# The turn between the second and the third stage of an FFT convolution: inside SBUF from GpSimd's queue instead of through DRAM

## The chip, the cores and the metric

One core of one Trainium2 chip. The metric is the device time of one execution in microseconds, and the runs of a kernel are compared by their median. "The profile" is one execution as the hardware profiler recorded it: a summary page, and a trace that can be asked for groups of instructions, waits, transfers and stretches of time. Engines: PE is TensorE (PEld its weight loads), DVE is VectorE, ACT is ScalarE, POOL is GpSimd, SP is SyncE; SPq, ACTq and POOLq are the sequencers of those engines when they only issue a transfer.

## The reference

Shapes: `u` is 2048 x 512 (time by channel), 512 channels with 128 states each, a hidden layer of 1792. All float32.

```python
x = A_u
g = sigmoid((x * gate_w).sum(-1, keepdims=True))
# a: a long convolution per channel, with a kernel made of 128 complex exponentials
dt = exp(log_dt)[:, None]
P = exp(dt * (A_re + 1j*A_im))[..., None] ** arange(L)
K = einsum("dn,dnl,dn->dl", C_re + 1j*C_im, P, dt * (B_re + 1j*B_im)).real
a = irfft(rfft(u, 2*L) * rfft(K, 2*L))[:L] + u * Dskip
# b: a dense layer with gelu, and one back
b = gelu(x @ w1 + b1) @ w2 + b2
return g * a + (1 - g) * b
```

## The kernel before, in words

The work has two parts. The first, `front` (0 to 397 us), makes the convolution kernel's samples, takes the first stage of the Fourier transforms of signal and kernel into DRAM (`tu_d`, `tk_d`), and computes the dense branch, whose gated results are added into the output in DRAM. A planner orders its instructions. Two of the sixteen row tiles of the dense branch (the last N_LATE = 2 of the block treated last, tiles 2 and 3) are not finished there: their 14 groups of three products (a product with the high parts, and two with the low parts) are kept in the list `late`.

The second, `conv` (from 397 us), has an order written out by hand. It treats 32 frequencies, two in each of 16 steps `s`. In a step:

- `product(s)`: six VectorE operations multiply the transformed signal (`pu`, in PSUM) by the transformed kernel (`k0`, `k1`, in SBUF).
- `signal(s+1)` and `taps(s+2)`: eight TensorE products each for the coming steps; ScalarE copies the taps out of PSUM.
- `inverse(s)`: eight TensorE products (line 1158) give `pa`, for each of the two frequencies `n` a tile of 128 rows by 512 channels. A row is one of 64 samples, real or imaginary.
- `turn(s)`: ScalarE copies `pa` to one of six tiles `sa` in SBUF (line 1164), and the turn begins.

The turn exchanges rows for columns. The third stage sums over frequencies, so the frequencies have to lie on partitions: `t3` has 128 partitions (32 frequencies, real and imaginary, two halves) of 32 samples x 512 channels, 64 KB each. Before the change the turn goes through DRAM: SP writes each `sa` into `t4_d` (line 1167, 256 KB), and after every GROUP = 8 frequencies GpSimd's queue reads the group back into 32 partitions of `t3`, in four transfers of 512 KB (line 1176). The last group is read back in eight transfers of 256 KB from SP and ACT, and the write of frequency 31 is issued by ACT.

`seat(n)` says on which partition frequency `n` sits; the constants (`g1` for the third stage, `g2` for the inverse stage) are laid out to fit. `matrices(m)` makes from a loaded constant tile the second set of weights (`f1`, `g1`) with four ScalarE instructions (lines 1103 to 1106); it serves two steps.

While the steps run, `fetch` and `load_u` load the taps and the signal (SP), and from step 6 on `dense(k)` loads the dense results of output block k back from DRAM (SP, line 1186, 512 KB).

Behind step 15:

- `rest(n)` issues the next `n` groups of the late list (lines 1197 to 1199). One group (N_REST) stands ahead of the last `inverse`, 13 behind it.
- A dummy product (`warm`, line 1235), then for the two late tiles a VectorE operation that gates and adds them (line 1239).
- Eight final blocks, one for each pair of output tiles `m`: sixteen TensorE products (line 1247) with the weights `g1t` give two PSUM tiles `pb`. A block reads four of the 32 samples of all the partitions of `t3`, so it needs every frequency, but of each only an eighth of its row. Eleven of the sixteen tiles are gated and added to the dense result by VectorE in one operation (line 1258); five (those in ASIDE) by ScalarE (line 1255) and GpSimd (line 1256). Each pair is then stored: 512 KB from SP (line 1262), the first and the last pair in two halves (line 1260).

Waits are put in by the framework from what the instructions read and write.

Of the kernel before, what the change touches and what calls it, by code (L numbers as in the profile page):

```python
# [9 lines left out]
F32 = mybir.dt.float32  # L10
# [3 lines left out]
ALU = mybir.AluOpType  # L14
# [3 lines left out]
P = 128  # L18
L = 2048
# [51 lines left out]
D_COE = 1.413  # L71
D_OUT = -13.28
N_REST = 1
N_KEEP = 1
N_PASS = 20
N_LATE = 2

N_ATTIC, N_LOFT, N_TK = 11, 8, 8
N_US = N_ATTIC + N_LOFT
W_DVE = ((1, 0), (3, 0), (5, 0))  # L80

GROUP = 8

ASIDE = (2, 4, 7, 9, 12)
PI = float(np.pi)
TWO_PI = 2.0 * PI
TURN = 2.0**32
# [13 lines left out]
    return [8 * (n % 4) + n // 4 for n in range(32)]  # L101


def seat(n):

    return 4 * (n % 8) + n // 8


def constants():


    def om(e4):
# [12 lines left out]


    rows = np.zeros((2, 64, 32))
    for n, k in enumerate(k0_order()):
        rows[:, seat(n)] = er.T[k] / L
        rows[:, seat(n) + 32] = ei.T[k] / L  # L130
    g1 = rows.reshape(P, 32)

    ko = k0_order()
    f2 = np.zeros((32, 2, 64, 64))
    g2 = np.zeros((32, 64, 64, 2))
    for n, k in enumerate(ko):
        er, ei = om(4 * (q[:, None] * k + 32 * np.outer(q, k1)) + q[:, None])
        f2[n, 0], f2[n, 1] = er, -ei  # L140
        er, ei = om(4 * (qn[None] * k + 32 * np.outer(k1, qn)) + qn[None])
        g2[n, :, :, 0], g2[n, :, :, 1] = er, -ei
# [153 lines left out]
def gated_mix(  # L296
# [21 lines left out]
    dr = ctx.enter_context(tc.tile_pool(name="dr", bufs=1, space=DRAM))  # L318

    dt_d = dr.tile([1, D], F32, name="dt_d")  # L320
    t4_d = dr.tile([4, 2, 2, GROUP, 32, D], F32, name="t4_d")
    tu_d = dr.tile([2, 32, 2, 64, D // 2], F32, name="tu_d")
    tk_d = dr.tile([2, 32, 2, 64, D // UW, 64], F32, name="tk_d")

# [753 lines left out]
    def conv(pool, ps, late, attic, loft):  # L1078
# [17 lines left out]
        def matrices(m):  # L1096

            cc = c4s[m]
            f = cc[:, 0].rearrange("p (n k) -> p n k", n=4)
            f1 = pool.tile([P, 4, 64], F32, tag="f1", name=f"f1{m}", bufs=2)  # L1100
            g = cc[:, 1].rearrange("p (s q c) -> p s q c", s=2, c=2)
            g1 = pool.tile([P, 2, 64, 2], F32, tag="g1", name=f"g1{m}", bufs=2)
            nc.scalar.mul(f1[0:64], f[64:128], -1.0)
            nc.scalar.copy(f1[64:128], f[0:64])
            nc.scalar.mul(g1[:, :, :, 0], g[:, :, :, 1], -1.0)
            nc.scalar.copy(g1[:, :, :, 1], g[:, :, :, 0])
            mats[m] = (f, f1), [z.rearrange("p s q c -> p s (q c)") for z in (g, g1)]

# [51 lines left out]
        def turn(s):  # L1160

            for n in (2 * s, 2 * s + 1):
                sa = sas[n % 6]
                nc.scalar.copy(sa, pas.pop(n))  # L1164
                g, k = divmod(n, GROUP)
                on = nc.sync if n < 31 else nc.scalar
                on.dma_start(t4_d[g, :, :, k].rearrange("i c q d -> q (i c) d"), sa)
                if k < GROUP - 1:
                    continue
                rows = t4_d[g].rearrange("i c k q d -> (i c k) q d")  # L1170


                w = 8 if n < 31 else 4
                for h in range(0, 32, w):
                    on = nc.gpsimd if n < 31 else (nc.scalar, nc.sync)[h // w % 2]
                    on.dma_start(t3[g:P:4, h : h + w], rows[:, h : h + w])

        accs, mos = {}, {}

# [32 lines left out]
        for s in range(16):  # L1212
# [15 lines left out]
            turn(s)  # L1228
            if 6 <= s < 14:
                dense(s - 6)  # L1230
        rest(14)

        warm = ps.tile([P, D], F32, tag="pa", name="warm", bufs=2)
        for _ in range(N_KEEP):
            nc.tensor.matmul(warm[0:64], mats[7][0][1][:, 3], zs[0], start=True, stop=True)
        for s in range(N_LATE):
            n = NT - N_LATE + s
            z = mos[n // 2][:, n % 2]
            nc.vector.scalar_tensor_tensor(z, accs[n], gate[:, 1, n : n + 1], z, ALU.mult, ALU.add)

        for m in range(8):
            tag, n = ("pa", 2) if m % 3 == 2 else ("pu", 4)
            pbs = [ps.tile([P, D], F32, tag=tag, name=f"pb{m}{i}", bufs=n) for i in range(2)]
            for b in range(4):
                for i in range(2):
# [4 lines left out]
            for i in range(2):  # L1250
# [5 lines left out]
                    nc.gpsimd.tensor_add(z, z, a)  # L1256
                else:
                    nc.vector.scalar_tensor_tensor(z, pbs[i], g, z, ALU.mult, ALU.add)
                if m in (0, 7):
                    (nc.sync, nc.scalar)[i if m else 0].dma_start(ov[m, :, i], z)  # L1260
            if 0 < m < 7:
                nc.sync.dma_start(ov[m], mos[m])

    ctx.enter_context(tc.manual_schedule())
    keep = ctx.enter_context(tc.tile_pool(name="keep", bufs=1))
# [75 lines left out]
```

## Time and profile before

| | us |
|---|---|
| three runs | 518.16, 517.01, 517.41; median 517.41 |
| the profiled execution | 515.96 |
| its span (first to last instruction) | 514.2 |
| granted TensorE clock, mean | 0.992 of full |
| busy in the span | PE 497.0, PEld 351.8, DVE 427.7, ACT 353.2, POOL 38.7 |
| moved by DMA | 101.26 MB, 197 GB/s on average |
| `turn`: 32 writes of 256 KB, median time to landing (31 from SP) | 5.2 |
| `turn`: 12 read-backs of 512 KB from GpSimd's queue, median time to landing | 6.9 |

How to read it: a row of the list in order of time gives start, duration, engine, line, operation, output<-input, shapes and count, and in brackets how long the engine was idle before it and what ended that. A group's row gives busy time and mean duration in ns behind the bar, then idle time. A row of the transfers gives the size of one and the median us from issue to landing. A row of waits gives us in total, times, and the longest. The times are those of one profiled execution, so sums are made against its span.

### The profile page before, as it was taken

The page shows a single profiled execution, that of the slowest core. Times are in us where ns is not written, and L with a number is a line of the kernel's source. Part 1 is how long each engine was busy: PE and PEld are TensorE (multiplying, and loading weights), DVE is VectorE, ACT ScalarE, POOL GpSimd, SP SyncE. Part 2 cuts the span into 40 slices and gives each one's busy share as a digit, 9 for nine tenths or more (in the row PEclk, how much of TensorE's full clock was granted, in tenths as well). Part 3 has the DMA queues.
Part 4 walks back from the last instruction along what each step waited for, and adds up shares of the span by engine and source line. Part 5 has one row for each costly group of instructions (what it writes and reads, how often), then busy time and mean ns, then how long its engine had stood idle before and what let it go on. Part 6 is the DMA issues. An engine that isn't in the chain of part 4 may idle for free.

```text
span 514.2 us, 11207 instructions
## 1 busy us (share of the span) xinstructions
PE 497.0 (97%) x4426; PEld 351.8 (68%) x4426; DVE 427.7 (83%) x794; ACT 353.2 (69%) x545; POOL 38.7 (8%) x74
## 2 busy tenths in 40 slices
PE   8998999989999999999999999999999999999992
PEld 5876787877777878788788888788787533333460
DVE  5989999989999999999999999999711675675533
ACT  6897959499995999977389958686354555555311
POOL 1000000000000000002300310002000001010113
PEclk9998999999999999999999999999999999999998
DMA  8989725172175727433950531716628999999977
GB/s 285 329 287 350 262 88 207 61 222 78 46 243 203 184 88 231 134 101 90 270 114 3 165 42 22 167 23 143 160 56 222 302 329 330 383 396 353 339 281 288
DMA packets 86805, 101.26 MB, mean 197 GB/s; under 512 B 38609, under 2 KB 58129, under 8 KB 86113
## 3 DMA queue, kind: packets, MB, share of 16 engines
q1 hardware_dynamic: 81216, 84.52, 49.8%
q0 software_dynamic: 5056, 14.45, 12.0%
q10 hardware_dynamic: 480, 1.57, 0.8%
q8 instruction: 35, 0.57, 0.5%
q14 instruction: 18, 0.14, 0.1%
HBM read 59.11 MB, written 41.42 MB: 196 GB/s over the span
## 4 chain that ended last, share of the span: by engine, by line
PE 64%; DVE 14%; issue 7%; ACT 7%; DMA 5%; SPq 1%; POOL 1%; POOLq 0%; DVEq 0%; ACTq 0%
PE pz L710 9%; PE ph L900 7%; PE ph L901 7%; PE ph L902 7%; PE acc L946 6%; PE acc L948 6%; PE acc L947 6%; PE p2k L1119 6%; PE p2u L1119 5%; PE pa L1158 5%; PE pz L426 2%; DVE y L675 2%; DVE y L688 2%; DVE loft L521 2%; DVE loft L520 1%
## 5 line engine op out<-in xcount | busy, mean ns | idle before, releaser
L900 PE MATMUL ph<-xh,wh 128*128 128x512 f32 x224 | 89.7, 400 | 1.7 <-ACT io L919 1.7
L901 PE MATMUL ph<-xlo,wh 128*128 128x512 f32 x224 | 88.2, 394 | 0.5 <-DVE xlo L827 0.4
L902 PE MATMUL ph<-xh,wl 128*128 128x512 f32 x224 | 88.0, 393 | 0.0
L946 PE MATMUL acc<-wh,hh 128*128 128x512 f32 x210 | 84.1, 400 | 0.7 <-ACT acc L952 0.7
L948 PE MATMUL acc<-wh,hl 128*128 128x512 f32 x210 | 82.1, 391 | 0.0
L947 PE MATMUL acc<-wl,hh 128*128 128x512 f32 x210 | 81.9, 390 | 0.0
L919 ACT ACTIVATE io<-ph,b1t 128x512 f32<-128x512 f32 x56 | 38.6, 690 | 34.8 <-PE ph L902 29.4
L710 PE MATMUL pz<-y,xc 128*32 128x64 f32 x2048 | 61.6, 290 | 0.4 <-DVE phase L620 0.4
L710 PEld LDWEIGHTS pz<-y,xc 128*32 128x32 f32 x2048 | 57.2, 136 | 6.7 <-issue 3.3
L928 DVE TENSOR_TENSOR hl<-io,hh 128x512 fp32r<-128x512 f32 x56 | 38.5, 687 | 22.7 <-ACT hh L920 22.5
L900 PEld LDWEIGHTS ph<-xh,wh 128*128 128x128 f32 x224 | 42.4, 189 | 14.3 <-ACT io L919 3.4
L901 PEld LDWEIGHTS ph<-xlo,wh 128*128 128x128 f32 x224 | 42.5, 190 | 10.4 <-DVE xlo L827 1.7
L946 PEld LDWEIGHTS acc<-wh,hh 128*128 128x128 f32 x210 | 39.4, 188 | 13.6 <-issue 3.8
L902 PEld LDWEIGHTS ph<-xh,wl 128*128 128x128 f32 x224 | 42.3, 189 | 9.2 <-DVE wl L827 0.3
L675 DVE TENSOR_TENSOR y<-y,ea 128x64 f32<-128x64 f32 (+4 forms) x80 | 45.3, 566 | 0.7 <-POOL y L665 0.4
L948 PEld LDWEIGHTS acc<-wh,hl 128*128 128x128 f32 x210 | 39.4, 188 | 9.0 <-DVE hl L928 0.5
L947 PEld LDWEIGHTS acc<-wl,hh 128*128 128x128 f32 x210 | 39.5, 188 | 7.7
L960 ACT ACTIVATE io<-acc,gate 128x512 f32<-128x512 f32 x30 | 20.3, 686 | 28.9 <-PE acc L948 28.9
L520 DVE TENSOR_TENSOR loft<-xc,zz 128x256 f32<-128x256 f32 (+2 forms) x48 | 37.3, 776 | 0.4
L521 DVE TENSOR_TENSOR loft<-xc,zz 128x256 f32<-128x256 f32 (+2 forms) x48 | 37.2, 774 | 0.0
L1141 DVE TENSOR_TENSOR v<-p2u,k 128x512 f32<-128x512 f32 x16 | 11.1, 691 | 31.1 <-ACT sa L1164 25.3
L688 DVE TENSOR_TENSOR y<-y,loft 128x2048 f32<-128x2048 f32 x16 | 36.6, 2285 | 0.2
(139 smaller groups left out, 840.1 us busy)
## 6 DMA issues: line engine op xcount, KB each, us to landing
tu_d<-attic SPq DMA_DIRECT2D x16, 512.0 KB, 3.5
tk_d<-sk SPq DMA_DIRECT2D x16, 512.0 KB, 6.8
tk<-tk_d SPq DMA_DIRECT2D x32, 256.0 KB, 5.9
t_d<-sa SPq DMA_DIRECT2D x31, 256.0 KB, 5.2
t<-t_d POOLq DMA_DIRECT2D x12, 512.0 KB, 6.9
attic<-tu_d SPq DMA_DIRECT2D x22, 256.0 KB, 4.7
attic<-in_xt_dram SPq DMA_DIRECT2D x20, 256.0 KB, 4.1
attic<-in_xs_dram SPq DMA_DIRECT2D x16, 256.0 KB, 5.3
```

Of the source, the lines that this page charges most:

```text
L520: vec(2 * m, lambda: vv.tensor_mul(t, a, br), due, [ka, *kb], [kt])
L521: vec(2 * m, lambda: vv.tensor_mul(v, a, bi), due, [ka, *kb], [kv])
L675: nc.vector.tensor_mul(both(n, 64 - 3 * n, n), both(0, 64 - n, n), an)
L688: v.tensor_mul(y[:, 0].rearrange("p (a b) c -> p a b c", a=2), e.rearrange("p (a b) c -> p a b c", a=2), cc,)
L710: nc.tensor.matmul(pk[32 * j : 32 * j + 32, gg // 4, gg % 4], x[:, r, :, ch], y[:, r, :, ch], start=(r == 0), stop=(r == 1), skip_group_ch ...
L900: nc.tensor.matmul(phs[q], h, xh[d], start=(d == 0), stop=False)
L901: nc.tensor.matmul(phs[q], h, xlo[d], start=False, stop=False)
L902: nc.tensor.matmul(phs[q], lo, xh[d], start=False, stop=(d == 3))
L946: nc.tensor.matmul(a, h, wh[1][f], start=(f == 0 and u >= NSB), stop=False, skip_group_check=True)
L947: nc.tensor.matmul(a, h, wl[1][f], start=False, stop=False, skip_group_check=True)
L948: nc.tensor.matmul(a, l, wh[1][f], start=False, stop=(f == FH - 1), skip_group_check=True)
L1119: nc.tensor.matmul(out[64 * i : 64 * i + 64], w, x, start=True, stop=True)
```

## The change

The turn no longer goes through DRAM: `t4_d` is gone. For each of the first 30 frequencies GpSimd's queue issues two transfers from `sa` (64 rows of 2 KB, 128 KB) straight into two whole partitions of `t3`, 16 apart. The last two frequencies go by quarters of `sa` (32 rows, 64 KB), each into four partitions, 32 apart, a quarter of their length: quarters 0 and 2 of frequency 30 from SP, those of 31 from ACT, quarters 1 and 3 of both from GpSimd. The copy of frequency 31 out of PSUM moves from ScalarE to VectorE. `seats()` and the constants change to fit, and with them the shapes in `matrices`; in `matrices(7)`, where the two layouts meet, two ScalarE instructions become four.

The end is ordered anew. The dummy product is gone. Of the 13 groups of the late list that stand behind the last `inverse`, five stay ahead of the final blocks, three go behind the first block, three behind the third, two behind the fifth (N_FIRST). The block that holds the late tiles (`m` = 1) comes last, and their two gated additions stand behind the sixth block. The tiles that ScalarE and GpSimd treat are others (ASIDE), five as before.

```diff
+N_FIRST = (5, 3, 0, 3, 0, 2, 0, 0, 0)
-GROUP = 8
+LATE = NT * (BLOCK[-1] + 1) - N_LATE
-ASIDE = (2, 4, 7, 9, 12)
+ASIDE = (5, 7, 9, 11, 13)
-def seat(n):
-    return 4 * (n % 8) + n // 8
+def seats():
+    free = [[y + d for y in range(4 * c, 4 * c + 4) for d in (0, 32) if y < 15] for c in range(4)]
+    to = []
+    for n in range(30):
+        c = n % 4 if free[n % 4] else max(range(4), key=lambda c: len(free[c]))
+        y = free[c].pop(0)
+        to.append((y, y + 16))
+    return [*to, (15, 47), (31, 63)]
...
-    t4_d = dr.tile([4, 2, 2, GROUP, 32, D], F32, name="t4_d")
...
-            nc.scalar.mul(g1[:, :, :, 0], g[:, :, :, 1], -1.0)
-            nc.scalar.copy(g1[:, :, :, 1], g[:, :, :, 0])
+            for s in ((slice(0, 2),) if m < 7 else (slice(0, 1), slice(1, 2))):
+                q = 8 if m == 7 and s.start else 32
+                a, b = (z[:, s].rearrange("p s (a c q) -> p (s a) c q", c=2, q=q) for z in (g, g1))
+                nc.scalar.mul(b[:, :, 0], a[:, :, 1], -1.0)
+                nc.scalar.copy(b[:, :, 1], a[:, :, 0])
...
                 sa = sas[n % 6]
-                nc.scalar.copy(sa, pas.pop(n))
-                g, k = divmod(n, GROUP)
-                on = nc.sync if n < 31 else nc.scalar
-                on.dma_start(t4_d[g, :, :, k].rearrange("i c q d -> q (i c) d"), sa)
-                if k < GROUP - 1:
-                    continue
-                rows = t4_d[g].rearrange("i c k q d -> (i c k) q d")
-                w = 8 if n < 31 else 4
-                for h in range(0, 32, w):
-                    on = nc.gpsimd if n < 31 else (nc.scalar, nc.sync)[h // w % 2]
-                    on.dma_start(t3[g:P:4, h : h + w], rows[:, h : h + w])
+                if n < 31:
+                    nc.scalar.copy(sa, pas.pop(n))
+                else:
+                    nc.vector.tensor_copy(sa, pas.pop(n))
+                y, z = seats()[n]
+                if n < 30:
+                    for i in range(2):
+                        r = slice(64 * i, 64 * i + 64)
+                        nc.gpsimd.dma_start(t3[64 * i + y : 64 * i + z + 1 : 16], sa[r])
+            if s == 15:
+                for h in range(4):
+                    for n in (30, 31):
+                        y = seats()[n][0]
+                        on = nc.gpsimd if h % 2 else (nc.sync, nc.scalar)[n % 2]
+                        on.dma_start(t3[y:P:32, 8 * h : 8 * h + 8], sas[n % 6][32 * h : 32 * h + 32])
...
-        rest(14)
-        warm = ps.tile([P, D], F32, tag="pa", name="warm", bufs=2)
-        for _ in range(N_KEEP):
-            nc.tensor.matmul(warm[0:64], mats[7][0][1][:, 3], zs[0], start=True, stop=True)
-        for s in range(N_LATE):
-            n = NT - N_LATE + s
-            z = mos[n // 2][:, n % 2]
-            nc.vector.scalar_tensor_tensor(z, accs[n], gate[:, 1, n : n + 1], z, ALU.mult, ALU.add)
-        for m in range(8):
-            tag, n = ("pa", 2) if m % 3 == 2 else ("pu", 4)
+        rest(N_FIRST[0])
+        late_m = LATE // 2
+        order = [m for m in range(8) if m != late_m] + [late_m]
+        for k, m in enumerate(order):
+            tag, n = ("pa", 2) if k % 3 == 2 else ("pu", 4)
...
+            rest(N_FIRST[k + 1])
+            if k == 5:
+                for i in range(N_LATE):
+                    z, g = mos[late_m][:, i], gate[:, 1, LATE + i : LATE + i + 1]
+                    nc.vector.scalar_tensor_tensor(z, accs[NT - N_LATE + i], g, z, ALU.mult, ALU.add)
```

More of the change, by code (lines that the diff above doesn't have):

```diff
@@ L73 @@
 N_REST = 1
-N_KEEP = 1
 N_PASS = 20
 N_LATE = 2
+N_FIRST = (5, 3, 0, 3, 0, 2, 0, 0, 0)
 N_ATTIC, N_LOFT, N_TK = 11, 8, 8
@@ L127, in constants @@
     rows = np.zeros((2, 64, 32))
-    for n, k in enumerate(k0_order()):
-        rows[:, seat(n)] = er.T[k] / L
-        rows[:, seat(n) + 32] = ei.T[k] / L
+    for (y, z), k in zip(seats(), k0_order()):
+        rows[:, y] = er.T[k] / L
+        rows[:, z] = ei.T[k] / L
     g1 = rows.reshape(P, 32)
@@ L136, in constants @@
     f2 = np.zeros((32, 2, 64, 64))
-    g2 = np.zeros((32, 64, 64, 2))
+    g2 = np.zeros((32, 64, P))
     for n, k in enumerate(ko):
@@ L141, in constants @@
         er, ei = om(4 * (qn[None] * k + 32 * np.outer(k1, qn)) + qn[None])
-        g2[n, :, :, 0], g2[n, :, :, 1] = er, -ei
+        g = np.stack([er, -ei], 2).reshape(64, 4, 8, 2, 2)
+        g2[n] = g.transpose(0, 3, 4, 1, 2).reshape(64, P) if n < 30 else g.transpose(0, 1, 3, 4, 2).reshape(64, P)
     f2 = f2.reshape(8, 4, P, 64).transpose(0, 2, 1, 3).reshape(8, P, 256)
@@ L1100, in matrices @@
             f1 = pool.tile([P, 4, 64], F32, tag="f1", name=f"f1{m}", bufs=2)
-            g = cc[:, 1].rearrange("p (s q c) -> p s q c", s=2, c=2)
-            g1 = pool.tile([P, 2, 64, 2], F32, tag="g1", name=f"g1{m}", bufs=2)
+            g = cc[:, 1].rearrange("p (s n) -> p s n", s=2)
+            g1 = pool.tile([P, 2, P], F32, tag="g1", name=f"g1{m}", bufs=2)
             nc.scalar.mul(f1[0:64], f[64:128], -1.0)
             nc.scalar.copy(f1[64:128], f[0:64])
-            nc.scalar.mul(g1[:, :, :, 0], g[:, :, :, 1], -1.0)
-            nc.scalar.copy(g1[:, :, :, 1], g[:, :, :, 0])
-            mats[m] = (f, f1), [z.rearrange("p s q c -> p s (q c)") for z in (g, g1)]
+            for s in ((slice(0, 2),) if m < 7 else (slice(0, 1), slice(1, 2))):
[3 more added lines that the diff above has]
+                nc.scalar.copy(b[:, :, 1], a[:, :, 0])
+            mats[m] = (f, f1), (g, g1)
         fac, pus, prod, pas = {}, {}, {}, {}
@@ L1258, in conv @@
                     nc.vector.scalar_tensor_tensor(z, pbs[i], g, z, ALU.mult, ALU.add)
-                if m in (0, 7):
-                    (nc.sync, nc.scalar)[i if m else 0].dma_start(ov[m, :, i], z)
-            if 0 < m < 7:
+                if k in (0, 7):
+                    (nc.sync, nc.scalar)[i if k else 0].dma_start(ov[m, :, i], z)
+            if 0 < k < 7:
                 nc.sync.dma_start(ov[m], mos[m])
+            rest(N_FIRST[k + 1])
[3 more added lines that the diff above has]
+                    nc.vector.scalar_tensor_tensor(z, accs[NT - N_LATE + i], g, z, ALU.mult, ALU.add)
     ctx.enter_context(tc.manual_schedule())
```

## The prediction

> **What bounds the kernel now.** I read the stages first (busy time by stretch), then the chain that ended last and the waits inside the frequency stage, then the list in order of time from 482 us on, and last the transfers of that stretch. Columns of the first view: stretch in us, its length, busy us and count of PE, PEld, DVE, ACT, POOL, then granted clock, DMA share, GB/s.
>
> ```profile
> 425.00:450.00 25.00, 25.00 (x112) 8.05 (x112) 16.45 (x27) 14.07 (x30) 2.10 (x4) 1.00 1.01 357
> 417.74 1.92 PE pa L1158 x8
> 419.65 1.87 PE p2u L1119 x8
> 421.52 1.72 PE p2k L1119 x8
> PE p2k L1119 <- DMA tk<-tk_d: 0.2, 1, 0.2
> ```
>
> TensorE is busy in all 25 us of a stretch in the middle of the frequency stage, at clock 1.00, and a step is three pieces of it: 1.92 + 1.87 + 1.72 = 5.51 us. DMA is as full (share 1.01), but TensorE waits for a transfer only 0.2 us in the whole stage. So the frequency stage is a TensorE stage, and fewer bytes in it are worth nothing by themselves. What can move is what comes after the last step:
>
> ```profile
> 484.03 1.07 ACT L1164 COPY sa<-pa 128x512 f32<-128x512 f32 x2 [2.75 <-issue]
> 486.86 1.07 ACT L1164 COPY sa<-pa 128x512 f32<-128x512 f32 x2 [1.75 <-issue]
> 487.07 0.50 PE L1197 MATMUL acc<-wh,hh 128*128 128x512 f32 x1
> 487.96 0.63 ACTq L1167 DMA_DIRECT2D t_d<-sa  x1
> 492.07 2.59 ACTq L1176 DMA_DIRECT2D t<-t_d  x4
> 495.82 0.39 PE L1199 MATMUL acc<-wh,hl 128*128 128x512 f32 x1
> 496.14 1.07 PE L1235 MATMUL warm<-z,f 128*64 128x512 f32 x2
> 497.14 7.17 PE L1247 MATMUL pb<-t,g1t 64*32 64x512 f32 x128
> 498.32 2.73 DVE L1258 SCALAR_TENSOR_TENSOR loft<-pb,gate,loft 128x512 f32<-128x512 f32 x4 [1.32 <-PE pb L1247]
> 500.96 5.09 DVE L1258 SCALAR_TENSOR_TENSOR attic<-pb,gate,attic 128x512 f32<-128x512 f32 x7
> 503.74 2.98 SPq L1262 DMA_DIRECT2D out_dram<-attic  x4
> 506.08 0.41 ACTq L1260 DMA_DIRECT2D out_dram<-attic  x1
> 506.81 1.12 SPq L1260 DMA_DIRECT2D out_dram<-attic  x1
> ```
>
> The last two frequencies are copied out by 487.93. They go to DRAM (ACT's issue at 487.96) and come back (ACT's first read-back at 492.07). TensorE fills that time with the 13 remaining groups of three dense products, 487.07 to 496.14, 0.69 us a group (9.07/13 = 0.698, the first one is slow), then with a dummy product, and runs the eight final blocks from 497.14 in one piece, 7.17/8 = 0.90 us a block, to 504.31. VectorE combines results from 498.32 to 506.05 without a gap (5.09/7 = 0.73 us each), and the stores follow.
>
> ```profile
> t<-t_d ACTq DMA_DIRECT2D x1, 256.0 KB, 3.7
> out_dram<-loft SPq DMA_DIRECT2D x2, 256.0 KB, 2.3
> out_dram<-loft SPq DMA_DIRECT2D x1, 512.0 KB, 2.8
> out_dram<-attic ACTq DMA_DIRECT2D x1, 256.0 KB, 6.0
> out_dram<-attic SPq DMA_DIRECT2D x1, 256.0 KB, 6.3
> 508.00:510.00 2.00, 0.00 (x0) 0.00 (x0) 0.00 (x0) 0.00 (x0) 0.00 (x0) 0.78 1.03 395
> ```
>
> The numbers at the end are us from issue to landing. The first read-back lands at 492.07 + 3.7 = 495.8, so the final blocks could not have begun earlier than that. A first 256 KB store lands in 2.3 us on a free DMA, the last one in 6.3 because 2 MB stand ahead of it and DMA is full (395 GB/s). It lands at 506.81 + 6.3 = 513.1, and the span ends at 514.2: 1.1 us behind. The end is thus set by two things together: when the final blocks may start, and how many bytes are pushed out behind the last of them.
>
> **The change, part by part.** *The frequency stage.* Gone are 31 SP and 1 ACT issues to DRAM, 12 POOL, 4 SP and 4 ACT read-backs. New are 60 POOL issues of 128 KB (two for each of the first 30 frequencies) and 8 of 64 KB for the last two (four POOL, two SP, two ACT).
>
> ```profile
> 239.81 2.14 POOL L847 DMA_DIRECT2D xh<-xh_d  x4
> L971 POOL DMA_DIRECT2D out_dram<-io x2 | 1.7, 954 | 29.4 <-ACT io L960 29.4
> DMA to landing us min/median/max: 2.7/5.2/10.2
> L1105 ACT ACTIVATE g<-cc 128x128 f32<-128x128 f32 x8 | 2.6, 326 | 0.2
> ACT sa L1164 <- PE pa L1158: 17.4, 14, 1.3
> ```
>
> POOL's issue: 2.14/4 = 0.53 us for 256 KB in 128 rows, 0.95 us at worst (the accumulating ones). A step issues four, 2.1 us (3.8 at worst) in 5.51: POOL has nothing else there, so the cost is zero. It would show only if an issue took over 1.38 us. The ring of six `sa` tiles: a copy overwrites what the transfer of three steps earlier reads, 16.5 us back; the transfers out of `sa` (the row of landings is that of line 1167) took 5.2 us in the median and 10.2 at most, so ScalarE does not wait, at zero. SP no longer stops for ScalarE's copies, so its loads go earlier; TensorE waited 0.2 us for them, so at most that is won; I take zero. The inner DRAM round trip of 512 KB out and 512 KB back a step becomes 512 KB inside SBUF; DMA has slack, TensorE sets the step, zero. `matrices(7)` has four column operations on ScalarE in place of two; each costs 0.33 us at full size, so under 0.66 us are added once, beside ScalarE's idle time (17.4 us before 14 of its `sa` copies, up to 1.3 a step), zero. If these covers failed, each would lengthen one step by its own size.
>
> *When the final blocks may start.* TensorE's order up to 487.07 is unchanged. Frequencies 28 and 29 are ready at 484.6 and 485.1 (two copies from 484.03); POOL issues their four transfers in 2.1 us from 484.7, the last at 486.3. Frequency 31 is now copied by VectorE beside ScalarE's copy of 30.
>
> ```profile
> 491.49 0.75 DVE L1239 SCALAR_TENSOR_TENSOR loft<-acc,gate,loft 128x512 f32<-128x512 f32 x1 [6.51 <-PE acc L1199]
> 496.25 0.75 DVE L1239 SCALAR_TENSOR_TENSOR loft<-acc,gate,loft 128x512 f32<-128x512 f32 x1 [4.01 <-PE acc L1199]
> L1142 DVE TENSOR_TENSOR v<-p2u,k 128x512 f32<-128x512 f32 x16 | 10.9, 680 | 0.0
> t_d<-sa SPq DMA_DIRECT2D x2, 256.0 KB, 2.7
> t_d<-sa SPq DMA_DIRECT2D x2, 256.0 KB, 5.1
> 482.07 0.55 SPq L1186 DMA_DIRECT2D attic<-out_dram  x1
> ```
>
> VectorE is idle there (6.51 us before 491.49). Its copy starts some 0.28 us after the last product (487.07), takes 0.68 as its reads of PSUM do, and is ready at 488.0, where ScalarE's second copy ended at 487.93: no gain. The quarters that the first two final blocks read then leave from SP at 487.5 and from ACT at 488.0. No transfer from SBUF into two or four partitions of SBUF stands in this trace. The nearest rows are the transfers from the same `sa` to DRAM: 2.7 us at best, 5.1 at 484.64, 5.2 in the median, 10.2 at worst. I take 5.2 for the last POOL transfer, since it carries half the bytes but lands in two partitions only: 486.3 + 5.2 = 491.5. The quarter on ACT takes 2.7 to 3.7 (the free-DMA rows above), landing by 491.7. The dense load of 482.07 is done by then, and the 2 MB of grouped read-backs no longer run beside it. So S, the start of the final blocks, is 491.5. Its floor is TensorE's own work, 487.07 + 5 x 0.69 = 490.5; its ceiling 486.3 + 10.2 = 496.5.
>
> [...]
>
> *From S to the end.* The dummy product goes (1.07 us of TensorE, already hidden behind the move of S). The 13 groups are split: 5 before S, 3 behind block 1, 3 behind block 3, 2 behind block 5. TensorE: 8 x 0.90 + 8 x 0.69 = 12.7 us, S + 12.7 = 504.2, as before (504.31). The groups still run somewhere; only their place changes. The sixth block in order (rows of m=6) starts at S + 5 x 0.90 + 8 x 0.69 = S + 10.0 and ends at S + 10.9 = 502.4; VectorE starts on it 0.28 us later at 502.7 and has seven operations left: one of m=6, the two gated additions of the late dense tiles (at 491.49 and 496.25 before, in idle time, now in this queue, +1.5 us), two of m=7, two of m=1. 7 x 0.73 = 5.1: it ends at 507.8, against 506.05 before: 1.7 us **later**. ScalarE (0.69) and POOL (1.26) finish the other half of m=6 at 504.8.
>
> ```profile
> 499.95 2.52 POOL L1256 TENSOR_TENSOR loft<-loft,sa 128x512 f32<-128x512 f32 x2 [21.34 <-ACT sa L1255]
> 500.04 0.69 ACT L1255 ACTIVATE sa<-pb,gate 128x512 f32<-128x512 f32 x1 [0.17 <-PE pb L1247]
> ```
>
> But the stores are spread out. From 503.74 before, four of 512 KB and two of 256 KB (2.62 MB) were issued; now from 504.8 come 512 (m=6), 512 at 506.3 (m=7), 256 at 507.1 and 256 at 507.8 (m=1): 1.57 MB. Floor: the last lands 2.3 us after its issue, 510.1. Ceiling: the old queue, 513.1 - 503.74 - 2.62/0.395 = 2.7 us of latency, plus 1.57/0.395 = 4.0, from 504.8: 511.5. I take the middle, 510.8, because these come 0.7 to 1.5 us apart, between the two templates. Plus 1.1: the span ends at **511.9**, 2.3 us less. The profiled execution took 515.96 us (span 514.2 plus 1.8); it becomes 513.7. The median of the runs, 517.41, lies 1.45 above that execution, and the same 2.3 taken from it give **515.1 us**.
>
> **The rivals.** (A) *The transfers land earlier*, at 2.7 us: S is TensorE's floor 490.5 and the last store takes 2.3: VectorE ends 506.8, the span 510.2, 4.0 less: 513.4 us. For it: DMA has half the turn's bytes and no reads beside it after 488. Against it: only two destination partitions a transfer.
>
> (B) *The transfers land late* (slower). The two-partition transfers of frequencies 28 and 29 become the wait that takes the place of the read-back. All behind S moves one for one, so it decides from S = 491.5 + 2.3 = 493.8, that is 7.5 us from the last POOL issue (and is measurable 1 us later). At 10.2 us, S = 496.5, 5.0 later: span 516.9, 520.1 us. For it, a row of this very stretch, and 64 KB must pass into one partition:
>
> ```profile
> t<-t_d ACTq DMA_DIRECT2D x2, 256.0 KB, 6.5
> ```
>
>  Against it: those 6.5 us are of the read-backs, which queue on each other; here little else is queued.
>
> (C) *The change does not do what it says*: the direct transfers land so late that the saved round trip is just paid back, 6.5 to 8.5 us after the last issue, S 492.8 to 494.8, 516.4 to 518.4 us.
>
> (D) *Too few DMA engines carry the turn.* If a transfer into two partitions used two engines and always the same ones, four of 128 KB at 49 GB/s take 10.6 us a step, 5.1 over the 5.51: ScalarE would wait for `sa`, TensorE for ScalarE, some 15 x 5.1 = 76 us, 591 us. It decides below four engines in use (99 GB/s, 5.3 us a step). Nothing in the trace shows such a transfer. [...]
>
> **How the numbers follow.** A measurement of this kernel tells 0.2% (1 us) from no change. My case (S 490.9 to 492.7) 0.51, A 0.16, C 0.13, B (S over 494.8) 0.16, D 0.04. Mine and A are faster, C is within 0.2%, B and D are slower: 0.67, 0.13, 0.20. The range goes from A, 513.4, to where B begins, S 495: 518.6; D and the worst of B (under 2 in 10) stay out. Mine alone, by S, reaches from 514.5 to 516.3.
>
> **What the profile afterwards would show.** Steps of 5.51 us and the last inverse product ending at 487.1, as now: D is out. POOL issues of 0.5 us, four a step. The first final block at 491 to 492, ended by a DMA landing or by nothing; at 490.5 it is A, past 493.8 it is B. TensorE's blocks in four clusters, ending 12.7 us after S. VectorE's last operation near 507.8, with the two late additions among its last seven. The last store landing 2.3 to 3.7 us after its issue; if it takes 6 again, the spread of the stores was worth nothing and I am wrong by 2.3 to 3 us. What would make me wrong most easily is the landing of a transfer into two partitions, which no row prices.

## The result, and the profile after

| | runs | median us | span us of the profiled execution |
|---|---|---|---|
| before | 4 | 517.21 (516.83 to 518.16) | 514.2 |
| after | 4 | 599.21 (594.42 to 600.08) | 598.3 |

The change makes the kernel slower: ratio 1.1563, 95% interval 1.15 to 1.1626. The forecast was 515.1, so the sign was wrong and the time lies far outside the range (513.4 to 518.6). It lies beside rival D, priced at 591 us and given 4 in 100.

The page of the kernel after. First its span, then two groups of instructions (busy us and mean ns of one behind the bar, then the idle time before them and what ended most of it), then GpSimd's DMA queue (packets, MB, share of 16 engines' time) and its row of transfers (KB of one, median us to landing).

```profile
span 598.3 us, 11213 instructions
L1174 ACT COPY sa<-pa 128x512 f32<-128x512 f32 x31 | 17.9, 587 | 94.3 <-DMA t<-sa 67.2
L1181 POOL DMA_DIRECT2D t<-sa x60 | 40.0, 668 | 128.6 <-issue 117.4
q0 software_dynamic: 21120, 16.40, 13.9%
t<-sa POOLq DMA_DIRECT2D x60, 128.0 KB, 7.5
```

The copies out of PSUM that cost ScalarE 17.9 us now stand behind 94.3 us of waiting, 67.2 of them for transfers out of `sa`. And GpSimd, priced at zero, stands 117.4 us at "issue": it waits in front of a transfer for nothing that the profile shows. Its order of time shows how that begins (start, duration, count, idle time before):

```profile
411.11 2.11 POOL L1181 DMA_DIRECT2D t<-sa  x3 [10.84 <-ACT sa L1174]
421.46 0.66 POOL L1181 DMA_DIRECT2D t<-sa  x1 [8.24 <-issue]
423.12 0.66 POOL L1181 DMA_DIRECT2D t<-sa  x1 [0.99 <-issue]
...
568.18 0.66 POOL L1181 DMA_DIRECT2D t<-sa  x1 [3.49 <-issue]
569.02 2.35 POOL L1187 DMA_DIRECT2D t<-sa  x4 [0.18 <-issue]
```

Three transfers go out back to back, 2.11 us for three. The fourth goes out only 8.24 us later, although its tile had long been copied, and from then on they go almost singly. An issue itself takes 0.67 us. The list of waits gives the chain that grows out of it (total us, times, longest):

```profile
POOL t L1181 <- issue: 117.4, 53, 8.2
ACT sa L1174 <- DMA t<-sa: 67.2, 16, 7.9
DVE v L1150 <- PE p2u L1128: 73.1, 12, 11.2
```

GpSimd waits before 53 of 60 transfers; so tiles `sa` come free late; so ScalarE waits 16 times, up to 7.9 us; so TensorE's products come late, and VectorE waits 73.1 us for them. By stretch (us, length, busy us and count of PE, PEld, DVE, ACT, POOL, then clock, DMA share, GB/s):

```profile
411.00:440.00 29.00, 25.85 (x110) 7.77 (x106) 18.42 (x30) 11.21 (x24) 6.11 (x9) 1.00 1.09 256
440.00:480.00 40.00, 28.65 (x78) 7.95 (x78) 11.24 (x18) 10.82 (x23) 9.98 (x15) 0.74 0.59 153
520.00:560.00 40.00, 28.63 (x76) 11.42 (x74) 8.06 (x13) 5.67 (x10) 11.29 (x17) 0.70 0.32 74
```

This view is the one to remember. Up to 440 the six tiles still cover most of it, and TensorE is busy 25.85 of 29 us. From 440 on nothing is full: TensorE 28.65 of 40 us at a clock of 0.74 and then 0.70, DMA 0.59 and then 0.32 of its time, 153 and 74 GB/s. In this stage no engine and no DMA is full, and one queue stands at "issue": what it is short of is no engine. VectorE's first product of a step starts at 402.2, 405.8, 411.1, 416.6, 422.1 and 427.6 us (5.5 us apart from the third on, as before), and from there 7.4, 13.9, 9.0, 14.9, 8.4, 9.2, 14.4, 6.2, 13.9 and 5.6 apart.

The end, in order of time:

```profile
548.83 2.76 PE L1167 MATMUL pa<-v,g 64*128 64x512 f32 x3
574.01 3.54 PE L1252 MATMUL pb<-t,g1t 64*32 64x512 f32 x16 [17.45 <-DMA t<-sa]
592.18 1.40 DVE L1263 SCALAR_TENSOR_TENSOR loft<-pb,gate,loft 128x512 f32<-128x512 f32 x2
```

The last inverse product ends at 551.6 (before: 487.1), the final blocks start at S = 574.0, 22.4 us behind it (before: 10.1), and the span ends 24.3 us after S (before: 17.1). So of the 84.1 us of span, 64.5 were lost in the frequency stage, 12.3 between it and the final blocks, and 7.2 in the end.

### The profile page after: what moved, and what is told of

Read it like the earlier page. It is cut to its first block, busy times and chain, and to the rows that moved or that the text cites. A ratio compares the mean times of both kernels' runs of the same rounds, so it can differ in the third digit from the quotient of the medians.

```text
span 598.3 us, 11213 instructions
## 1 busy us (share of the span) xinstructions
PE 528.0 (88%) x4424; PEld 357.0 (60%) x4424; DVE 428.6 (72%) x795; ACT 352.5 (59%) x546; POOL 75.1 (13%) x126
## 3 DMA queue, kind: packets, MB, share of 16 engines
q0 software_dynamic: 21120, 16.40, 13.9%
## 4 chain that ended last, share of the span: by engine, by line
PE 44%; issue 17%; DVE 13%; ACT 10%; DMA 10%; POOL 4%; SPq 1%; DVEq 0%; POOLq 0%; ACTq 0%
PE pz L716 7%; DMA t<-sa 5%; PE ph L906 5%; PE ph L907 5%; PE ph L908 5%; PE acc L952 5%; PE acc L954 5%; PE acc L953 5%; POOL t L1181 4%; PE p2k L1128 2%; PE pz L432 2%; DVE loft L527 2%; DVE y L694 1%; DVE loft L526 1%; DVE y L681 1%
## 5 line engine op out<-in xcount | busy, mean ns | idle before, releaser
L952 PE MATMUL acc<-wh,hh 128*128 128x512 f32 x210 | 84.1, 401 | 0.8 <-ACT acc L958 0.8
L1174 ACT COPY sa<-pa 128x512 f32<-128x512 f32 x31 | 17.9, 587 | 94.3 <-DMA t<-sa 67.2
L1150 DVE TENSOR_TENSOR v<-p2u,k 128x512 f32<-128x512 f32 x16 | 11.1, 691 | 78.4 <-PE p2u L1128 73.1
L1181 POOL DMA_DIRECT2D t<-sa x60 | 40.0, 668 | 128.6 <-issue 117.4
L1167 PE MATMUL pa<-v,cc 64*128 64x512 f32 x64 | 31.1, 781 | 20.7 <-ACT sa L1174 20.7
L907 PEld LDWEIGHTS ph<-xlo,wh 128*128 128x128 f32 x224 | 42.5, 190 | 10.2 <-DVE xlo L833 1.5
L526 DVE TENSOR_TENSOR loft<-xc,zz 128x256 f32<-128x256 f32 (+2 forms) x48 | 37.2, 775 | 0.4
```

Source lines behind the costliest of these rows:

```text
L526: vec(2 * m, lambda: vv.tensor_mul(t, a, br), due, [ka, *kb], [kt])
L907: nc.tensor.matmul(phs[q], h, xlo[d], start=False, stop=False)
L952: nc.tensor.matmul(a, h, wh[1][f], start=(f == 0 and u >= NSB), stop=False, skip_group_check=True)
L1181: nc.gpsimd.dma_start(t3[64 * i + y : 64 * i + z + 1 : 16], sa[r])
```

## The experiments

Two theories stood at the start, both of them guesses. **Room** (R; "the ring" in the expectations): the kernel gives GpSimd's transfers a limited room, SCRATCH, only three of these transfers fit into it, and the fourth issue waits for a landing. **Place** (P): two partitions of SBUF take data slowly, whoever sends it. Rivals to both: too few DMA engines carry the bytes (E), the issuing queue (GpSimd) is slow, or DMA as a whole is full. All times are medians beside a run of the kernel before on the same chip (516.3 to 517.0 us); a single run where no interval is given.

### The room

```diff
-SCRATCH = 2048
+SCRATCH = 1024
```

SCRATCH is what the kernel passes as `dynamic_dma_scratch_size` (line 1333), in bytes.

> The changed kernel with half the room for GpSimd's transfer descriptors (SCRATCH 1024 instead of 2048 bytes a partition). [...] Theory E (too few DMA engines carry the bytes, the queue on GpSimd is only their backlog): no change, 599 us, steps of 10.5.

814.7 us; the room theory, with one transfer in flight, had asked for 800 to 900. The other side, with one `io` tile less in the front part to make room:

```diff
-N_ACC, N_H, N_IO = 2, 2, 3
-SCRATCH = 2048
+N_ACC, N_H, N_IO = 2, 2, 2
+SCRATCH = 4096
```

> The changed kernel with twice the room for descriptors (SCRATCH 4096); the room comes from N_IO, two buffers in place of three in the first part, which may cost that part up to 3 us (seen in when it ends, 397 us). [...] Theory E: the same bytes over the same engines, steps of 10.5, 599 us.

562.8 us, ratio 1.0893 (1.0842 to 1.0944). The rows for the direct transfers: issue min/median/max in ns, then first and last start in us. First scratch1024, with its waits and its landing, then scratch4096 with the same and, in a fence of its own, its order of time. After's issues go from 411.11 to 568.18 (shown above).

```profile
L1181 POOL DMA_DIRECT2D t<-sa x60: 662/667/747, 410.6 to 782.9; - x60
POOL t L1181 <- issue: 332.7, 59, 9.8
t<-sa POOLq DMA_DIRECT2D x60, 128.0 KB, 5.7
```

```profile
L1181 POOL DMA_DIRECT2D t<-sa x60: 662/662/738, 417.8 to 527.6; - x60
POOL t L1181 <- DMA t<-sa: 35.0, 22, 6.8
POOL t L1181 <- issue: 28.2, 15, 3.7
t<-sa POOLq DMA_DIRECT2D x60, 128.0 KB, 13.2
```

```profile
405.31 1.73 POOL L977 DMA_DIRECT2D out_dram<-io  x2 [32.60 <-ACT io L966]
417.82 2.75 POOL L1181 DMA_DIRECT2D t<-sa  x4 [10.78 <-ACT sa L1174]
423.24 1.99 POOL L1181 DMA_DIRECT2D t<-sa  x3 [2.67 <-ACT sa L1174]
427.90 0.66 POOL L1181 DMA_DIRECT2D t<-sa  x1 [2.67 <-DMA t<-sa]
```

The stretch from the first to the last issue of the direct transfers (the turn, below) takes 372 us with 1 KB, 157 with 2 KB and 110 with 4 KB. In the first, GpSimd waits before 59 of 60 issues: one transfer is in flight. With 2 KB three are; with 4 KB seven go out (4 + 3, held up only by ScalarE) before the first wait for a landing, at 427.90: the eighth, whose tile the seventh had already used. That is the room, by dose: one and seven in flight was also the room theory's forecast. If each transfer takes the same room, an estimate from these counts is between 512 and 585 bytes of the scratch (seven fit into 4096; a second does not fit into 1024). And the step follows as four transfers times landing over number in flight: 4 x 5.7 / 1 = 23 us, 4 x 7.5 / 3 = 10.0 us, 4 x 13.2 / 7 = 7.5 us, against measured means of 25.2, 10.7 and 7.4 (the turn over its 59/4 steps). Of the 562.8 us, about 6.8 belong to the smaller `io` pool, not to the turn: GpSimd's last store of the front part starts at 405.31 in place of 398.53.

But the landing grew with the number in flight, 5.7, 7.5, 13.2. So with 4 KB GpSimd still waits before 37 of its 60 issues: 28.2 us at "issue" and 35.0 us for landings of its own transfers. The steps take 7.4 us, and the forecast of 512 to 520 us, which left the landing at 7.5, missed by over 40. Why a transfer takes 13.2 us there is the second question.

### The queue that issues

```diff
-                        nc.gpsimd.dma_start(t3[64 * i + y : 64 * i + z + 1 : 16], sa[r])
+                        nc.sync.dma_start(t3[64 * i + y : 64 * i + z + 1 : 16], sa[r])
```

> [...]

661.0 us, where the room theory had asked for 515 to 540 and E for 595 to 620: worse, so it does not help to take the transfers off GpSimd's queue (that this queue can carry them is shown by the run "flat" below). From its page and its stretches:

```profile
q0 software_dynamic: 4800, 8.43, 6.7%
...
455.00:485.00 30.00, 16.52 (x48) 5.65 (x48) 6.46 (x12) 6.00 (x12) 0.00 (x0) 0.72 0.35 105
```

DMA is busy 0.35 of its time, at 105 GB/s. In the trace's packets, the 60 transfers add 120 of 4 bytes to SP's queue, two each. And in this stretch one or two of the 2 KB pieces on SP's queue, most of them the turn's, are under way at once in 0.90 of the time. (In the kernel after, from 440 to 470 us, two to four 4 KB pieces of GpSimd's transfers are, in 0.89 of the time.) TensorE now waits 54.2 us for the tap loads that go through the same SP queue. The time lies beyond rival D's price; few pieces are under way at once, but which engines carry them, no row names.

The packet counts tell where the transfers from GpSimd's queue differ. With the 60 transfers gone from it, q0 has 4,800 packets; in the kernel after it has 21,120, so one 128 KB transfer leaves 16,320 / 60 = 272. In the run "flat" below, which sends the same bytes to 64 partitions, it leaves (7,680 - 4,800) / 60 = 48: 32 of 4 KB and 16 of 4 bytes. The 224 more carry 0.11 MB in all (16.40 against 16.29 MB), 8 bytes each; the kernel before has no packet of 8 bytes on this queue. In the run "four" below, a transfer of 256 KB into four partitions leaves 272 as well ((12,960 - 4,800) / 30), and three are in flight again. So with 2 KB of scratch three fly where a transfer leaves 272 packets, of 128 KB as of 256, and flat's, with 48, are not held up (0.3 us at "issue"). What fills the room, and where the packets of 8 bytes come from, no run shows.

### The place of the destination

```diff
-                        nc.gpsimd.dma_start(t3[64 * i + y : 64 * i + z + 1 : 16], sa[r])
+                        nc.gpsimd.dma_start(t4_d[n // 8, i, :, n % 8].rearrange("c q d -> c (q d)"), sa[r])
```

on top of the 4 KB of scratch: the same 60 transfers end in two rows of 64 KB in DRAM.

> The changed kernel with SCRATCH 4096 (and N_IO 2), and the 60 transfers of the first 30 frequencies write two rows of 64 KB in DRAM instead of two partitions of t3; t3 is filled with zeros for them, so this part of the turn is left out. [...] Theory P (writing 64 KB into one partition collides with the loads that write all partitions, so that the DMA engines are occupied but slow: 220 GB/s at a share of 1.15): without that destination the DMA runs at 300 GB/s or more, steps of 5.5 us, 510 to 525 us. [...]

546.4 us; if the destination did not matter, 555 to 570 had been forecast. And the same 60 transfers, with 2 KB of scratch, into 64 partitions:

```diff
-                        nc.gpsimd.dma_start(t3[64 * i + y : 64 * i + z + 1 : 16], sa[r])
+                        nc.gpsimd.dma_start(t3[r, n], sa[r])
```

> The changed kernel (SCRATCH 2048) with the same 60 transfers of 64 rows from GpSimd's queue, but into 64 partitions, row by row (the turn itself is left out). [...] If GpSimd still waits and the steps stay over 6 us, the number of transfers or GpSimd's issue is the limit, and neither ring nor destination.

520.3 us (forecast by R with P: 512 to 518). One stretch of each, first scratch4096, then to_dram, then flat with its queue and its transfers:

```profile
455.00:485.00 30.00, 23.29 (x92) 6.81 (x88) 14.73 (x24) 8.53 (x17) 8.64 (x13) 0.95 1.16 223
```

```profile
455.00:485.00 30.00, 29.50 (x128) 9.00 (x126) 20.00 (x34) 15.00 (x31) 13.33 (x21) 1.00 0.90 251
```

```profile
q0 software_dynamic: 7680, 16.29, 14.6%
...
455.00:485.00 30.00, 30.00 (x133) 9.48 (x128) 20.88 (x35) 14.08 (x31) 11.79 (x24) 1.00 0.99 271
...
L1181 POOL DMA_DIRECT2D t<-sa x60: 516/523/566, 410.6 to 487.5; - x60
```

Flat has TensorE busy in all of the 30 us, as before: here direct transfers from GpSimd's queue cost the frequency stage nothing, spread over 64 partitions, and 2 KB of scratch is enough for them (0.3 us at "issue"). (The 3 us that flat lies above before are in the end, which is the new one here too; it is tried alone below.) To two partitions DMA is *more* busy (share 1.16) and moves *less* (223 GB/s) than flat (0.99 at 271); the same pieces to DRAM give 0.90 at 251. Why, no row shows. The loads beside them are slower too: the 4 KB packets of SP's loads (from 430 us to the last issue of the turn) take 258 ns in the median in scratch4096 and 159 in to_dram, as in the kernel before. to_dram starts its turn 11 us later than scratch4096, behind a memset of `t3` that stands in for the data left out, and still makes it in 84 us (428.6 to 512.9) against 110. Its time lies between the two forecasts, since GpSimd still waits: 13.4 us at "issue" and 26.6 for landings of 9.3 us.

In the kernel after itself, with three in flight, the destination hardly shows: the packets of SP's loads take 159 ns, those of its own transfers 165, and a transfer lands in 7.5 us where flat's lands in 7.1. What flat does not have is the wait at "issue" (0.3 us in place of 117.4).

### Four partitions, 32 or 8 apart

To move the place alone, one transfer of 256 KB takes each frequency to four partitions, first 32 apart (`seats()` changes to fit):

```diff
-                    for i in range(2):
-                        r = slice(64 * i, 64 * i + 64)
-                        nc.gpsimd.dma_start(t3[64 * i + y : 64 * i + z + 1 : 16], sa[r])
+                    nc.gpsimd.dma_start(t3[y:P:32], sa)
```

> The changed kernel with one transfer a frequency, all 128 rows of sa into four partitions 32 apart (256 KB), and seats and weights to fit; SCRATCH 2048 as in the changed kernel. [...]

579.2 us, ratio 1.122 (1.1197 to 1.1242). R and E had both asked for 513 to 522, and 599 would have spoken against both. Three are in flight as forecast, but each lands in 13.9 us and not in 7.5: two transfers a step make 2 x 13.9 / 3 = 9.3 us (measured 9.2). Then the same with 8 apart, for the quarters of the last two frequencies too:

```diff
-                    nc.gpsimd.dma_start(t3[y:P:32], sa)
+                    y = 32 * (n % 4) + n // 4
+                    nc.gpsimd.dma_start(t3[y : y + 25 : 8], sa)
```

> The kernel 'four' (one transfer of 256 KB a frequency into four partitions, SCRATCH 2048) with the four partitions 8 apart instead of 32 apart; the rows so land on other partitions than the third stage expects, which is left wrong. [...] If the destination's place does not matter (ring and engines alone): the same 575 to 582 us.

556.1 us (2 x 11.6 / 3 = 7.7 us a step, measured 7.7), with the same packets and bytes on GpSimd's queue (12,960 and 16.34 MB in both): better by 23 us, but short of what the place theory alone had asked for, 515 to 535. Both again with 4 KB of scratch and the smaller `io` pool:

> One 256 KB transfer a frequency into four partitions 32 apart, as in the run with 2 KB of scratch (579.2 us, GpSimd 102 us in front of these issues), now with 4 KB of scratch and two io tiles in place of three. The smaller io pool alone costs 6.8 us of the front part (GpSimd's last accumulating store at 405.3 against 398.5 us in the run of the change with 4 KB). Theory of two limits (ring and destination): with four partitions 32 apart the destination is the limit, so twice as many in flight only queue there: 570 to 590 us, landing 20 us or more, GpSimd's wait in front of the issue halved but ScalarE's wait for the transfers out of sa grown. Rival (the ring alone): as for the transfers into two partitions, where 4 KB took 36 us off: 535 to 550 us.

> The same, into four partitions 8 apart (rows misplaced, as in the run with 2 KB: 556.1 us, landing 11.6, GpSimd 72.7 us in front of its issues). Theory of two limits: here more in flight helps more than with partitions 32 apart: 530 to 550 us, of which 6.8 us are the io pool's. If the destination were no limit at all (the ring alone), the difference to the run with partitions 32 apart would go: both equal within 5 us. If 4 KB helps neither, the destination or the six sa tiles hold both, and the time is 556 to 565 us.

570.5 us (ratio 1.1048, 1.0986 to 1.111) and 551.1 us (1.0681, 1.0637 to 1.0726). Four kernels in the order four, four8, four4096, four8_4096: first and last issue of the turn, for the two at 32 apart GpSimd's main wait in front of it, and one stretch.

```profile
L1174 POOL DMA_DIRECT2D t<-sa x30: 685/685/737, 410.1 to 543.9; - x30
POOL t L1174 <- issue: 102.1, 22, 8.1
455.00:485.00 30.00, 21.34 (x80) 6.28 (x78) 11.05 (x18) 8.04 (x16) 3.43 (x5) 0.86 1.11 192
```

```profile
L1175 POOL DMA_DIRECT2D t<-sa x30: 688/688/741, 411.0 to 522.5; - x30
455.00:485.00 30.00, 20.20 (x72) 6.00 (x71) 11.05 (x18) 9.45 (x21) 4.83 (x7) 0.87 1.09 225
```

```profile
L1174 POOL DMA_DIRECT2D t<-sa x30: 687/687/740, 417.2 to 530.8; - x30
POOL t L1174 <- ACT sa L1169: 104.4, 19, 12.4
455.00:485.00 30.00, 20.44 (x62) 5.89 (x62) 10.10 (x18) 7.56 (x15) 3.47 (x6) 0.77 1.14 188
```

```profile
L1175 POOL DMA_DIRECT2D t<-sa x30: 691/691/743, 419.9 to 514.0; - x30
455.00:485.00 30.00, 25.29 (x88) 7.39 (x88) 12.71 (x21) 10.54 (x22) 4.12 (x6) 0.89 1.11 239
```

With 4 KB the wait at "issue" is gone from both; GpSimd waits only for ScalarE's copies. The turn still takes 113.6 us at 32 apart and 94.1 at 8 apart (133.8 and 111.5 with 2 KB). So both limits are there, and nearly add up: the room is worth 20 and 17 us of the turn, the place 22 and 20. The room alone would have left the two 4 KB kernels equal; they differ by 19.4 us in the medians. The packets of 4 KB on GpSimd's queue take 341 ns in the median at 32 apart and 256 at 8 apart (348 and 286 with 4 KB of scratch), and those of SP's loads beside them 326 and 251 (305 and 249). GpSimd's own packets alone are no sure sign: 246 in scratch4096 and 159 in to_dram are medians, of which the means are 269 and 265, and flat's take 256 without harm. Not even 8 apart is free: with no wait at "issue" the turn is still 17 us longer than flat's 76.9 (410.6 to 487.5).

These four runs agree in direction, and the sizes are theirs alone; why 32 apart is slower than 8 apart, no row shows.

### The new order of the end, alone

The kernel before, with only the second half of the change (the 13 groups split, the block of the late tiles last, its additions behind the sixth block, no dummy product, other tiles aside):

```diff
+N_FIRST = (5, 3, 0, 3, 0, 2, 0, 0, 0)
-        rest(14)
-        warm = ps.tile([P, D], F32, tag="pa", name="warm", bufs=2)
+        rest(N_FIRST[0])
+        order = [m for m in range(8) if m != late_m] + [late_m]
...
+            rest(N_FIRST[k + 1])
```

> The kernel before, with its turn through DRAM, and only the new order of the end (five groups of late products first, the rest between the blocks, the late tiles last, other tiles aside, no dummy product). By the prediction's sum the span ends 20.4 us behind the start of the final blocks; here that start cannot come before the read-back lands at 495.8, and TensorE has nothing to do from 490.5 on: span 516.2, 2.0 us slower than before (519 us). Rival: the spread stores gain nothing, VectorE's later end counts in full: 3.5 to 5 us slower, or TensorE slows down after the gap.

522.05 us, ratio 1.01 (1.0081 to 1.0119). In order of time, with one stretch of it (the granted clock is the third number from the end):

```profile
490.10 0.39 PE L1200 MATMUL acc<-wh,hl 128*128 128x512 f32 x1
...
495.62 1.96 PE L1242 MATMUL pb<-t,g1t 64*32 64x512 f32 x16 [5.14 <-DMA t<-t_d]
497.51 0.79 PE L1198 MATMUL acc<-wh,hh 128*128 128x512 f32 x1
...
501.19 1.95 PE L1242 MATMUL pb<-t,g1t 64*32 64x512 f32 x32
...
495.60:500.20 4.60, 4.58 (x22) 2.40 (x23) 1.41 (x2) 0.00 (x0) 0.00 (x0) 0.50 0.86 314
...
513.31 1.40 DVE L1253 SCALAR_TENSOR_TENSOR loft<-pb,gate,loft 128x512 f32<-128x512 f32 x2
```

TensorE is done with its five groups at 490.5 and idles 5.14 us for the read-backs. Then it is slow: the first block takes 1.96 us in place of 0.90, the first products behind it 0.79 and 0.63 in place of 0.39; only from 501.19 on does a block take its 0.97. The granted clock is 0.50 in the slow stretch and 1.00 from 500.7 to 505. S itself is 1.5 us earlier than before (497.14), but the old order had filled this wait with work that had to be done anyway. From S = 495.62 the last VectorE operation ends at S + 19.1 and the span at S + 23.7 (519.3), where the prediction had S + 16.3 and S + 20.4. The slow stretch lasts 4.6 us (495.6 to 500.2). That this is about as long as the idle one ahead of it is no rule: in hybrid2 below TensorE is slow for 3.0 us behind 13.1 us of idling, in hybrid3 for 5.2 behind 9.5.

### Versions meant to win

If the fault lies in the many transfers, the old way for frequencies 0 to 27 and direct transfers for the last four should keep the gain at the end. Three tries, each in five rounds (the first one's edit, with an access pattern shortened):

```diff
+                    if n >= 28:
+                        nc.gpsimd.dma_start(t3[y:P:32], sa)
+                        continue
+                    nc.sync.dma_start(t4_d[g]..., sa)
```

> The changed kernel's end, and its direct turn only for the last four frequencies: 0 to 27 through DRAM (groups of 8, 8, 8 and 4), 28 and 29 as one transfer of 256 KB into four partitions each, 30 and 31 by quarters as in the change. Theory R with P: few direct transfers never fill the ring and meet few loads, steps stay 5.5 us, the final blocks start at 491.5 to 493.5, and by the prediction's sum it ends 1 to 2.5 us before the kernel before: 514.5 to 516.5 us. Rival: the landing of the direct transfers or of the last group stays over 8 us, the start is past 494, and it is no faster: 517 to 520 us.

578.4 us (ratio 1.1181, 1.1155 to 1.1206): a slip of mine, and a lesson. The DRAM side of the writes had an outermost size of 4 (four packets of 4 bytes to each write on SP's queue, sixteen in the next run), and the steps stretched up to 15.7 us, with DMA at 0.60 to 0.68 of its time (212 to 236 GB/s in three stretches from 425 to 515 us). I put it down to too few engines for a write, which no row shows. With 32 x 4 rows outermost, as the kernel before has it, and the group 24 to 27 read back behind the last step, by SP and GpSimd:

> [...] Frequencies 0 to 27 through DRAM, the last group of four read back by SP and GpSimd behind the direct transfers of 28 and 29, the end as in the change. If the number of engines was what held the first hybrid: steps of 5.5 us, last inverse product at 487, the final blocks start at 491.5 to 494, and with the 23.7 us from there to the end of the span that the run with the new end alone showed, less its slow start of TensorE (2.6 us), 513 to 515 of span, 514.5 to 517 us. Rival: the direct transfers land past 495, the start is no better than 496 to 497 and it is 1 to 3 us slower than the kernel before.

529.1 us (1.024, 1.0218 to 1.0263); and with nine groups kept ahead of the final blocks (N_FIRST = (9, 2, 0, 2, 0, ...)):

> As the second hybrid, with nine groups of late products ahead of the final blocks, two behind the first and two behind the third, and the two late additions behind the fourth block: TensorE has work until 493.4, does not idle and keeps its clock, and VectorE's last stretch has two operations less. Expected 512 to 515 us if the transfers land by 493.5; the rival (landing past 495) gives 516 to 519.

527.5 us (1.0208, 1.0187 to 1.0229). Both are slower than their forecasts and the rivals to them. The steps are 5.5 us again, and the loss has moved behind them. hybrid2's transfers issued from 480 to 512 us, then hybrid3's start of the final blocks and the stretch ahead of it:

```profile
t<-sa POOLq DMA_DIRECT2D x2, 256.0 KB, 10.5
t<-t_d SPq DMA_DIRECT2D x2, 256.0 KB, 12.1
t<-sa POOLq DMA_DIRECT2D x4, 64.0 KB, 14.2
```

```profile
503.30 1.96 PE L1269 MATMUL pb<-t,g1t 64*32 64x512 f32 x16 [9.49 <-DMA t<-sa]
...
490.00:500.00 10.00, 3.80 (x17) 2.82 (x15) 0.00 (x0) 0.00 (x0) 2.25 (x4) 0.91 0.84 161
```

Two direct transfers of 256 KB, the eight quarters and the four read-backs of the last group are enough: a read-back of 256 KB lands in 12.1 us (before: 3.7 and 6.5), a quarter of 64 KB takes 14.2, DMA is 0.84 busy at 161 GB/s, and S is 503.3 to 504.6 against 497.1 before. Which of the three holds up the others was not tried apart.

What remains is to take the dummy product out of the kernel before, and nothing else:

```diff
-        warm = ps.tile([P, D], F32, tag="pa", name="warm", bufs=2)
-        for _ in range(N_KEEP):
-            nc.tensor.matmul(warm[0:64], mats[7][0][1][:, 3], zs[0], start=True, stop=True)
```

> The kernel before without its dummy product between the late products and the final blocks. By its profile the first read-back lands at 495.8 and the late products end at 496.2, so the blocks can start at 496.2 instead of 497.14, and by the prediction's rule (all behind the start moves one for one) it ends 0.9 us earlier: 516.0 us, just within what a measurement tells. Rival: the read-backs of the later quarters or the stores set the end, or TensorE's clock drops without the dummy: 517 to 518.

515.89 against 516.97 us, ratio 0.9985 (0.9971 to 1.0): the fastest version measured, but the interval reaches from no gain to one of 1.5 us, so it can hardly be told from no change.

```profile
499.00 5.38 PE L1244 MATMUL pb<-t,g1t 64*32 64x512 f32 x96 [0.42 <-DMA t<-t_d]
```

The blocks start at 496.64, 0.5 us earlier than before, and the third then waits 0.42 us for a read-back: the dummy product had mostly covered a wait. The profiled span is 514.2 in both.

## Why the prediction was wrong, step by step

- **"POOL's issue ... the cost is zero. It would show only if an issue took over 1.38 us."** This step failed. The duration was nearly right (0.67 us for 0.53). But 0.53 came from transfers of 128 rows, in a trace whose queue has no packets of 8 bytes, and here GpSimd also waits in front of an issue: 117.4 us in 53 places, 332.7 us with 1 KB of SCRATCH and 28.2 with 4 KB. Nothing before the change showed it: a read-back there is 32 packets of 16 KB, and even flat, with the same queue and bytes as the kernel after, waits 0.3 us at "issue".
- **The ring of six `sa` tiles, "at zero".** Failed with it: 16.5 us were set against landings of 5.2 to 10.2. What counts is not the landing alone but the wait for the issue ahead of it; the two together ate the cover by the seventh step.
- **The landing of a two-partition transfer, 5.2 us.** Measured 7.5 in the median (5.4 at least with one in flight), 13.2 with seven, and 9 to 14 us for those into four partitions at the end of the hybrids. The text named this as what would make it wrong most easily; but it was priced once, at the end, as an addition to S, and not sixty times as a rate. With three in flight the landing of sixty transfers is a rate: 4 x 7.5 / 3 = 10.0 us a step (measured 10.7). At the end it was the backlog and not this landing that moved S: the last of the sixty was issued 16.6 us behind the last inverse product (568.18 against 551.6; forecast: 0.8 us ahead of it), and S came 5.8 us after that issue (forecast: 5.2).
- **"DMA has slack, TensorE sets the step, zero."** Wrong in kind, and against the prediction's own row, which had DMA as full (1.01): half the bytes left DMA neither idle nor fast. Bytes were not the currency; in scratch4096 the engines are 1.16 busy at 223 GB/s.
- **Rival D.** Nearest in number (591 us, 10.6 us a step; measured 599.2 and 10.7), at a chance of 0.04. Its 49 GB/s is an estimate, two sixteenths of the 395 GB/s of the last stores before; no run shows how many engines carry a transfer, or that they are always the same. What the runs show in its place is three transfers in flight (scratch1024 one, scratch4096 seven). That the two steps agree so well is luck: its 10.6 is four transfers one behind the other at 49 GB/s each, the measured 10.7 is three in flight that land in 7.5 us. Where the queue was not GpSimd's, in from_sp, the time was 661 us, beyond D's price.
- **The end.** S + 16.3 and S + 20.4 were too short by 2.8 and 3.3 us: end_only gives S + 19.1 and S + 23.7, after itself S + 19.6 and S + 24.3. The sum left out that TensorE restarts slowly (granted clock 0.50) behind a wait that the moved groups no longer fill: some 2.6 us of TensorE's 16.0 from S on (1.06 in the first block, 1.5 in the three groups behind it); the rest is about 0.7 us for switching between blocks and groups. Behind the 0.42 us of idling in no_warm a block takes its 0.90; whether the 1 us that was forecast ahead of S would have brought the slow restart, no run shows. Without it S + 21.1 remains, and the forecast's 2.3 us would have been 1.6.
- **Right:** `matrices(7)` costs nothing that shows, TensorE's blocks stand in four clusters, and the two late additions are among VectorE's last. In flat, with the frequency stage intact, the last inverse product ends at 488.1, within 1 us of the forecast's 487.1.

Open: how much the turn of the kernel after would lose to the destination if the room held it no longer. With two partitions the 4 KB of scratch took 47 us off the turn (157 to 110), and sending the same to DRAM another 26; but a room in which nothing waits was not tried with two partitions. And what makes 32 apart slower than 8 apart was not measured apart from the distance.

## What to carry to other kernels

Before many small direct transfers are moved to GpSimd's queue, find out how many of them it keeps in flight: here one, three and seven with 1, 2 and 4 KB of SCRATCH, for transfers into two partitions, while those into 64 did not wait. With so few, landing over number in flight became the step (23, 10.0 and 7.5 us; measured 25.2, 10.7 and 7.4). Several transfers in flight that end in two (4 KB of SCRATCH) or four partitions of SBUF slowed the loads beside them too (4 KB packets of 249 to 326 ns in place of 159); spread over 64 they cost the frequency stage nothing, and sent to DRAM they left the loads at 159 ns. And when work is moved out of a wait, price TensorE's slow restart behind the wait that is then empty (here 3 to 5 us at a granted clock of 0.50).

## What the runs showed that I had not expected

A transfer into two partitions leaves 272 packets on GpSimd's queue in place of flat's 48, 224 of them of 8 bytes. DMA was more than fully busy (1.11 to 1.16) while it moved little more than half of what it moved before (188 to 223 GB/s against 357 at 1.01): here the busy share of DMA told nothing of the bytes. Four partitions 8 apart in place of 32 are worth 23 us of 579. From SP the same transfers held back the loads beside them (54.2 us of TensorE's waiting), and one slip in the outermost size of the DRAM writes, hybrid against hybrid2, lay 49 us apart (hybrid2 also reads its last group back later).
